# Own products with values in three pieces, and all products with values a tick later

## The chip, the cores and the metric

The kernel runs on one core of a Trainium2 chip. A core has five engines that run beside each other, each with its own program: TensorE (PE, matmuls; its weight loads are shown apart as PEld), VectorE (DVE), ScalarE (ACT), GpSimd (POOL) and SyncE (SP, which here does nothing but issue DMAs). They wait for each other on semaphores. The metric is the device time of one execution in microseconds (us).

## The reference

Block-sparse attention for 4 batches and 8 heads, 768 tokens of width 64 in blocks of 32 (so 24 blocks), with three drawn blocks of keys for each block of queries and a window of one block; then a mixture of eight experts on its output, 3072 tokens of 512, one expert for each token.

```python
scores = scale * np.matmul(q, k.transpose(0, 1, 3, 2))
...
mask = np.abs(blk_i - blk_j) <= window
mask = mask | (blk_i == 0) | (blk_j == 0) | (blk_i == n_blocks - 1) | (blk_j == n_blocks - 1)
for qb in range(n_blocks):
    for kb in sampled_blocks[qb]:
        mask[qb * block:(qb + 1) * block, kb * block:(kb + 1) * block] = True
scores = np.where(mask, scores, -1000000000.0)
scores = scores - np.max(scores, axis=-1, keepdims=True)
attn = np.exp(scores)
attn = attn / (np.sum(attn, axis=-1, keepdims=True) + 1e-09)
return np.matmul(attn, v).astype(np.float32)
...
for e in range(E):
    mask = e_idx == e
    if not mask.any():
        continue
    h = np.maximum(x[mask] @ w1[e], 0.0)
    out[mask] = gate_w[mask, None] * (h @ w2[e])
```

## The kernel before

Attention comes first, then the experts, whose first groups are begun while attention ends.

*Tiles and items.* The first and the last block of queries see all keys; they are worked on as "dense" items (kind "d"), 8 for each half of the batches. The other 22 blocks make 11 pairs, so with two halves there are 22 tiles of 128 tokens: two blocks (n) of two batches (b), for 8 heads. Each tile is four items of kind "s", one for each n and b. A block of queries sees eight blocks of keys. Four of them it shares with the other block of its tile (first, last, and the two of the tile's own pair): their values are the "shared" ones. The other four (three drawn ones and the neighbour outside the pair) are its "own".

*Ticks.* All items stand in one list, and in each tick `t` every step of the pipeline works on the item that is `LAG` ticks back; `ORDER` says in which order the steps stand within a tick. The steps are letters:

- S: scores on TensorE (L532, for both batches at once); M: mask and least value on VectorE (L540); X: exponential on ScalarE (L548)
- T: transposition of the weights on TensorE (L557); A: its copy out of the PSUM bank on ScalarE (L562); with a tile's last item also the sums' spreading on VectorE (L566)
- W: products of weights and shared values on TensorE (L579), into a new bank; the loop has 16 matmuls with 64 columns of weights each
- V: the sums of the rows by heads (L572, another bank), then the products with own values (L588): 32 matmuls with 32 columns each, into the bank that W began, four of them (j) for each of 8 heads
- O: division by the sums on VectorE (L439 to L441), which frees both banks; Y: turning of the result on TensorE (L595) and its copy by ScalarE (L597); G: gate logits on TensorE (L605), and after them the routing

W, V, O, Y and G work once for each tile, with its last item. For sparse items the lags of W, V, O, Y and G are 5, 7, 8, 10 and 13. Dense items have lags of their own, with a step W of their own (L430, L432). The order of every engine's program is the order in which this loop writes it: nothing is put elsewhere afterwards. An engine that waits holds up all that stands behind it on that engine.

*Values.* Two buffers hold a tile's values in turn (`vbuf[g % 2]`). For tile g SP loads two new neighbouring blocks (L495, L496; the first pairs also L490 to L493), and the drawn blocks of the two queries' blocks, three each (L520); GpSimd copies what the tile before has already (L503). `VL`, `VS` and `VG` say when: so many ticks after the last item of tile g-2, which used the same buffer, and at which of the eight places of a tick. Places 0 to 6 stand ahead of the steps O, X, T, S, M, A and W, place 7 at the tick's end. The load of q for a tile (`KL`, L143) and the writing of finished rows (`XD`, L1235) go through SP too, at place 2 and place 7.

*Banks.* PSUM has eight banks; attention takes them from one pool of eight.

*Records.* The trace shows two matmul records for each fp32 matmul of the program, but one for each transposition, and as many weight loads.

Of the kernel before, what the change touches and what calls it, by code (L numbers as in the profile page):

```python
# [38 lines left out]
HB = 2  # L39
# [21 lines left out]
ADVANCE = (((2, 3), (6, 6), (7, 1)), ((0, 2), (1, 1), (6, 4)))  # L61
LHS = (6, 5)
LHS_DVE = (True, True)
CHOOSE = ((0, 2),)
# [1 line left out]

KL = (-2, 2)
QP = (-2, 2)
VL = (8, 1)
VS = (11, 7)  # L70
VG = ((9, 6), (10, 3))

# [16 lines left out]
def attention_moe(ctx, tc, kD, qD, qH, v0, v1, blocks, modality, w_gate, bias, w1, w2, out):  # L89
# [29 lines left out]
    with ExitStack() as actx:  # L119
# [459 lines left out]
                    nc.tensor.matmul(o[64 * b:64 * b + 64, D * h:D * h + D], lhsT=a[b][:, 8 * u + 4 + pr].rearrange("p n q -> p (n q)"),  # L579
                                     rhs=vg[:, 1, b * HD + D * h:b * HD + D * h + D], start=h == 0, stop=False, tile_position=(0, 64 * b))  # L580

        def weigh_own(g, o, a):
            vg = vbuf[g % 2]
            for h in range(H):
                pr, u = divmod(h, 2)
                for j in range(4):
                    b, n = divmod(j, 2)
                    nc.tensor.matmul(o[32 * j:32 * j + 32, D * h:D * h + D], lhsT=a[b][:, 8 * u + pr, n],  # L588
                                     rhs=vg[:, 2 * n, b * HD + D * h:b * HD + D * h + D], start=False, stop=h == H - 1, tile_position=(0, 32 * j))
# [690 lines left out]
        def do(op, it):  # L1280
# [29 lines left out]
            else:  # L1310
# [20 lines left out]
                elif (n, b) == (1, HB - 1):  # L1331
# [16 lines left out]
        with man:  # L1348
# [16 lines left out]
            while t < NI + LAG["s"]["G"] + 1 or fillers or slots_todo or choosers or early:  # L1365
                spot = 0
                for op in ORDER:
                    if op in "TSMAXOW":
                        hook(spot)
                        spot += 1  # L1370
                    for kind in "ds":
                        k = t - LAG[kind][op]
                        if 0 <= k < NI and items[k][0] == kind:
                            do(op, items[k])
                hook(7)
                if t >= NI:
                    tail[0], tail[1] = t >= NI + TAIL, t >= NI + LAG["s"]["V"]
# [66 lines left out]
```

## Time and profile before

| | us |
|---|---|
| median of 3 runs | 537.08 |
| lowest and highest of them | 534.24, 539.2 |
| the profiled execution, its own time | 536.03 |
| its span, first to last instruction | 534.3 |

The mean granted TensorE clock of the profiled execution is 0.987 of full speed. The second part of the page cuts the span into 40 slices of 13.4 us; a digit is the busy share in tenths:

```profile
PE   7999999998999999899999999999999999999995
PEld 5667776766778777788989898998989899898984
DVE  7995698683788999867997656556565655656553
ACT  4689877884988878835456554546555454655552
POOL 3577685574468884323155022030302203030213
PEclk9999999997999999899999999999999999999998
```

Attention takes the first 17 slices. There TensorE, VectorE and ScalarE are all busy most of the time, and behind it TensorE nearly alone. The row PEclk shows the granted clock.

A matmul's end is modelled in such a trace, so a busy TensorE may still lose time between matmuls of different shapes: what counts is the time from one start to the next.

### The profile page before, as it was taken

To read this page: it belongs to the slowest core of one execution; us is meant where nothing else is said; L and a number is where in the kernel's file an instruction comes from. 1 tells how busy PE (TensorE), PEld (TensorE's weight loads), DVE (VectorE), ACT (ScalarE), POOL (GpSimd) and SP (SyncE) were. 2 spreads that over 40 slices of the span, in tenths; PEclk is the share of its full clock that TensorE was granted. 3 is DMA by queue.
4 is the path that set the end of the run, shared out by engine and by line. 5 is a ranking of instruction groups with operands and counts; after the bars stand their busy time and mean duration, and the time that the engine had idled before them with its cause. 6 is when DMAs were issued, how large, how long until landed. Compare 5 with 4: busy or idle time off the path is not lost.

```text
span 534.3 us, 19017 instructions
## 1 busy us (share of the span) xinstructions
PE 514.9 (96%) x7298; PEld 436.1 (82%) x7298; DVE 377.2 (71%) x1139; ACT 335.2 (63%) x765; POOL 214.9 (40%) x451
## 2 busy tenths in 40 slices
PE   7999999998999999899999999999999999999995
PEld 5667776766778777788989898998989899898984
DVE  7995698683788999867997656556565655656553
ACT  4689877884988878835456554546555454655552
POOL 3577685574468884323155022030302203030213
PEclk9999999997999999899999999999999999999998
DMA  7995887898846798965888686676758677675840
GB/s 278 339 234 153 238 244 224 243 229 223 232 126 194 198 231 252 274 193 200 238 288 303 227 261 200 237 252 202 244 177 261 203 227 242 213 246 180 257 155 23
DMA packets 49443, 119.44 MB, mean 224 GB/s; under 512 B 7744, under 2 KB 8128, under 8 KB 49344
## 3 DMA queue, kind: packets, MB, share of 16 engines
q1 hardware_dynamic: 45248, 105.02, 64.5%
q0 software_dynamic: 4096, 13.12, 7.3%
q8 instruction: 59, 0.97, 0.8%
q14 instruction: 40, 0.33, 0.2%
HBM read 105.52 MB, written 12.86 MB: 222 GB/s over the span
## 4 chain that ended last, share of the span: by engine, by line
issue 40%; PE 39%; DVE 7%; DMA 6%; POOL 6%; SPq 2%; ACT 1%; POOLq 0%; DVEq 0%; ACTq 0%
PE bank L557 7%; PE bank L532 6%; PE bank L579 4%; PE bank L588 4%; POOL slot L735 3%; DMA out<-slot,si 2%; DMA slot<-kD 2%; PE bank L605 2%; POOL out L789 2%; PE bank L595 2%; DVE y L540 2%; PE bank L753 1%; PE bank L769 1%; PE bank L770 1%; PE bank L768 1%
## 5 line engine op out<-in xcount | busy, mean ns | idle before, releaser
L724 DVE TENSOR_TENSOR slot<-slot 128x1024 fp32r<-128x1024 f32 x99 | 123.1, 1248 | 89.3 <-ACT slot L721 87.5
L721 ACT CAST slot<-slot 128x1024 fp32r<-128x1024 f32 x104 | 108.1, 1048 | 102.1 <-PE bank L754 52.1
L753 PE MATMUL bank<-slot 128*128 128x256 f32 x384 | 108.4, 282 | 0.0
L755 PE MATMUL bank<-slot 128*128 128x256 f32 x384 | 107.8, 281 | 0.0
L754 PE MATMUL bank<-slot 128*128 128x256 f32 x384 | 107.7, 280 | 0.0
L789 POOL DMA_INDIRECT out<-slot,si x20 | 25.4, 1270 | 178.6 <-ACT slot L785 175.6
L548 ACT ACTIVATE a<-y,mn 128x256 f32<-128x256 f32 x176 | 88.7, 511 | 7.7 <-DVE mn L540 7.6
L768 PE MATMUL bank<-slot 128*128 128x512 f32 x192 | 76.6, 399 | 0.0
L769 PE MATMUL bank<-slot 128*128 128x512 f32 x192 | 75.9, 395 | 0.0
L770 PE MATMUL bank<-slot 128*128 128x512 f32 x192 | 75.8, 395 | 0.0
L753 PEld LDWEIGHTS bank<-slot 128*128 128x128 f32 x384 | 72.3, 188 | 0.6
L754 PEld LDWEIGHTS bank<-slot 128*128 128x128 f32 x384 | 72.1, 188 | 0.4
L755 PEld LDWEIGHTS bank<-slot 128*128 128x128 f32 x384 | 72.2, 188 | 0.0
L540 DVE CUSTOM_DVE_ANT_1 y<-bank,smask 128x256 f32<-128x256 f32 x176 | 66.3, 416 | 0.6 <-PE bank L532 0.2
L481 POOL COPY slot<-slot 128x128 f32 x264 | 63.9, 294 | 0.0
L562 ACT COPY at<-bank 128x512 f32<-128x512 f32 x88 | 50.6, 576 | 12.8 <-PE bank L557 12.7
L557 PE MATMUL bank<-ident,a 128*128 128x128 f32 x352 | 52.8, 284 | 0.6 <-ACT a L400 0.5
L503 POOL TENSOR_SCALAR slot<-slot 32x1024 f32<-32x1024 f32 x40 | 41.9, 1048 | 28.0 <-PE bank L588 10.2
L532 PE MATMUL bank<-slot,q_raw 64*32 64x256 f32 x1408 | 48.8, 382 | 1.1 <-DMA q_raw<-qH 0.7
L770 PEld LDWEIGHTS bank<-slot 128*128 128x128 f32 x192 | 36.1, 188 | 8.4
L557 PEld LDWEIGHTS bank<-ident,a 128*128 128x128 f32 x352 | 38.9, 142 | 4.7 <-ACT a L548 0.8
L769 PEld LDWEIGHTS bank<-slot 128*128 128x128 f32 x192 | 36.1, 188 | 7.8 <-DVE slot L724 0.4
(302 smaller groups left out, 855.4 us busy)
## 6 DMA issues: line engine op xcount, KB each, us to landing
slot<-w SPq DMA_DIRECT2D x100, 512.0 KB, 4.0
slot<-v SPq DMA_DIRECT2D x180, 128.0 KB, 4.0
x_d<-xr SPq DMA_DIRECT2D x22, 256.5 KB, 5.3
q_raw<-qH SPq DMA_DIRECT2D x22, 256.0 KB, 4.8
slot<-v SPq DMA_DIRECT2D x16, 256.0 KB, 4.9
slot<-kD SPq DMA_DIRECT2D x13, 256.0 KB, 4.2
slot<-v SPq DMA_DIRECT2D x4, 768.0 KB, 11.9
slot<-w SPq DMA_DIRECT2D x10, 256.0 KB, 5.1
```

Of the source, the lines that this page charges most:

```text
L532: nc.tensor.matmul(sp[u][32 * pr:32 * pr + 32, b * 256:(b + 1) * 256], lhsT=q[r, b * NPAIR + pr, n, :], rhs=kv[r, s0:s0 + 8, b, pr, :], st ...
L540: nc.vector.tensor_tensor_reduce(y[:, u, :].rearrange("p (s f) -> p s f", s=8), sp[u][:, b * 256:(b + 1) * 256].rearrange("p (s f) -> p s ...
L548: nc.scalar.activation(a[:, u, :], y[:, u, :], AF.Exp, bias=mn[:, u:u + 1], scale=-1.0, accum_out=total[:, u:u + 1])
L557: nc.tensor.transpose(tp[:, k:k + P], a[:, u, c * P:(c + 1) * P], ident)
L721: nc.scalar.copy(h, s)
L724: (eng or (nc.gpsimd if n in POOL_SPLITS else nc.vector)).tensor_tensor(l, s, h.bitcast(F32), ALU.subtract)
L753: nc.tensor.matmul(o, lhsT=h[:, fs], rhs=xh[g % 2][:, c, :], start=c == 0 and f % 2 == 0, stop=False)
L754: nc.tensor.matmul(o, lhsT=h[:, fs], rhs=xl[g % 2][:, c, :], start=False, stop=False)
L755: nc.tensor.matmul(o, lhsT=l[:, fs], rhs=xh[g % 2][:, c, :], start=False, stop=c == 3 and f % 2 == 1)
L768: nc.tensor.matmul(o, lhsT=hh[0][:, f, ts_], rhs=h[:, fs], start=f == 0, stop=False)
L769: nc.tensor.matmul(o, lhsT=hh[0][:, f, ts_], rhs=l[:, fs], start=False, stop=False)
L770: nc.tensor.matmul(o, lhsT=hl[f // 4][:, f % 4, ts_], rhs=h[:, fs], start=False, stop=f == 7)
```

## The change

Sparse items get a third step with values, U. Own products are divided by heads: heads 0 and 1 in step W behind the shared products, heads 2 and 3 in step U, and heads 4 to 7 in step V behind the row sums. The steps of a tile move a tick later: W from 5 to 6, U at 7, V from 7 to 8, O from 8 to 9, Y from 10 to 11. G stays at 13. The very last item keeps its old ticks (`LAST`), with U between W and V. The load of new neighbouring blocks moves from place 1 to place 7 of its tick, since V now reads the old ones within that tick. The number of matmuls, copies and DMAs is the same.

```diff
-LAG = {'d': {'S': 0, 'M': 1, 'X': 2, 'T': 4, 'A': 4, 'W': 7, 'O': 8, 'V': 101, 'Y': 11, 'G': 13}, 's': {'S': 0, 'M': 1, 'X': 2, 'T': 4, 'A': 4, 'W': 5, 'V': 7, 'O': 8, 'Y': 10, 'G': 13}}
-ORDER = 'OXTSMGVAYW'
+LAG = {'d': {'S': 0, 'M': 1, 'X': 2, 'T': 4, 'A': 4, 'W': 7, 'O': 8, 'V': 101, 'Y': 11, 'G': 13}, 's': {'S': 0, 'M': 1, 'X': 2, 'T': 4, 'A': 4, 'W': 6, 'U': 7, 'V': 8, 'O': 9, 'Y': 11, 'G': 13}}
+LAST = {'W': 5, 'U': 6, 'V': 7, 'O': 8, 'Y': 10}
+OWN = {'W': (0, 2), 'U': (2, 4), 'V': (4, 8)}
+ORDER = 'OXTSMGVUAYW'
...
-VL = (8, 1)
+VL = (8, 7)
...
-        def weigh_own(g, o, a):
+        def weigh_own(g, o, a, heads):
             vg = vbuf[g % 2]
-            for h in range(H):
+            for h in range(*heads):
...
                         sum_rows(sums.pop((m, half)), banks[m, half])
-                        weigh_own(half * NM + m, st[it], [ats[m, half, b_] for b_ in range(HB)])
+                    if op in OWN:
+                        weigh_own(half * NM + m, st[it], [ats[m, half, b_] for b_ in range(HB)], OWN[op])
...
-                        k = t - LAG[kind][op]
+                        k = t - LAG[kind].get(op, NEVER)
                         if 0 <= k < NI and items[k][0] == kind:
                             do(op, items[k])
+                    if op in LAST and t - LAST[op] == NI - 1:
+                        do(op, items[NI - 1])
```

In the changed file these lines stand three further on (L579 is L582 there, L588 is L591, L595 is L598).

On TensorE, for one full tile from its shared products on, the order before is this; the names are the bank written, the weights and the moving operand, the size is that of the output, and x is the number of equal matmuls in a row:

```order
L579 MATMUL bank<-slot,at 64x64 x16
L557 MATMUL bank<-ident,a 128x128 x4
L595 MATMUL bank<-ident,xr 128x128 x4
L557 MATMUL bank<-ident,a 128x128 x4
L532 MATMUL bank<-slot,q_raw 32x256 x16
L572 MATMUL bank<-rexp,fold 32x8 x4
L588 MATMUL bank<-slot,at 32x64 x32
L557 MATMUL bank<-ident,a 128x128 x8
L532 MATMUL bank<-slot,q_raw 32x256 x16
L605 MATMUL bank<-wg_raw,xT 64x8 x8
```

After the change the same engine reads, for the same stretch:

```order
L582 MATMUL bank<-slot,at 64x64 x16
L591 MATMUL bank<-slot,at 32x64 x8
L560 MATMUL bank<-ident,a 128x128 x4
L535 MATMUL bank<-slot,q_raw 32x256 x16
L591 MATMUL bank<-slot,at 32x64 x8
L598 MATMUL bank<-ident,xr 128x128 x4
L560 MATMUL bank<-ident,a 128x128 x4
L575 MATMUL bank<-rexp,fold 32x8 x4
L591 MATMUL bank<-slot,at 32x64 x16
L560 MATMUL bank<-ident,a 128x128 x4
L535 MATMUL bank<-slot,q_raw 32x256 x16
L608 MATMUL bank<-wg_raw,xT 64x8 x8
```

The 32 own matmuls stand in three places instead of one, and each of them has transpositions behind it; four more transpositions follow the gate's matmuls.

On SP, in the first half of attention, the DMAs from a writing of finished rows on are in this order before:

```order
L1235 DMA x_d<-xrd 128x513
L495 DMA slot<-v 32x1024
L496 DMA slot<-v 32x1024
L143 DMA q_raw<-qH 128x512
L512 TENSOR_LOAD rb_i
L520 ISA
```

and after the change:

```order
L1238 DMA x_d<-xrd 128x513
L146 DMA q_raw<-qH 128x512
L515 TENSOR_LOAD rb_i
L498 DMA slot<-v 32x1024
L499 DMA slot<-v 32x1024
L523 ISA
```

The two loads of new blocks, which wait for own products, now stand behind the load of q and the reading of the drawn blocks' numbers instead of ahead of them. On VectorE the division (L439 to L441) stands a tick later among the masks. GpSimd's order is the same in both.

More of the change, by code (lines that the diff above doesn't have):

```diff
@@ L58 @@
 DENSE_AFTER = (21, 29, 45, 47)
[L59 to L60 removed]
+LAG = {'d': {'S': 0, 'M': 1, 'X': 2, 'T': 4, 'A': 4, 'W': 7, 'O': 8, 'V': 101, 'Y': 11, 'G': 13}, 's': {'S': 0, 'M': 1, 'X': 2, 'T': 4, 'A': 4, 'W': 6, 'U': 7, 'V': 8, 'O': 9, 'Y': 11, 'G': 13}}
+LAST = {'W': 5, 'U': 6, 'V': 7, 'O': 8, 'Y': 10}
+OWN = {'W': (0, 2), 'U': (2, 4), 'V': (4, 8)}
+ORDER = 'OXTSMGVUAYW'
 ADVANCE = (((2, 3), (6, 6), (7, 1)), ((0, 2), (1, 1), (6, 4)))
+NEVER = 1000
 LHS = (6, 5)
@@ L1371, in attention_moe @@
                     for kind in "ds":
-                        k = t - LAG[kind][op]
+                        k = t - LAG[kind].get(op, NEVER)
                         if 0 <= k < NI and items[k][0] == kind:
                             do(op, items[k])
+                    if op in LAST and t - LAST[op] == NI - 1:
+                        do(op, items[NI - 1])
                 hook(7)
                 if t >= NI:
-                    tail[0], tail[1] = t >= NI + TAIL, t >= NI + LAG["s"]["V"]
+                    tail[0], tail[1] = t >= NI + TAIL, t >= NI + LAST["V"]
                     for _ in range(2):
```

## The prediction

> **What bounds the kernel now.** I read the page first, then the busy times by stage, then the chain of work that ended last in order of time, and last TensorE's two timelines (its matmuls, and its weight loads, where a wait shows before it shows on the matmuls).
>
> The page gives engines and DMA queues:
>
> ```profile
> PE 514.9 (96%) x7298; PEld 436.1 (82%) x7298; DVE 377.2 (71%) x1139; ACT 335.2 (63%) x765; POOL 214.9 (40%) x451
> ...
> q8 instruction: 59, 0.97, 0.8%
> ```
>
> TensorE is busy 96% of the span, and queue 8 brought 59 packets of code. The trace holds 7298 matmuls and as many weight loads; 14,596 over 59 is 247 for each packet. So q8 carries TensorE's own code, one packet for some 250 instructions.
>
> Attention fills some 195 us, up to its last own products (L588) at 230.29 (row below), the experts the rest. What a tile of 128 tokens costs there is read from the chain of work, in order of time (start, length, what), in a stretch where no piece waits:
>
> ```profile
> 165.24 0.98 PE bank L579 x32
> 166.22 0.59 PE bank L557 x4
> 166.81 0.44 PE bank L595 x4
> 167.25 0.44 PE bank L557 x4
> 167.68 1.02 PE bank L532 x32
> 168.71 0.18 PE bank L572 x8
> 168.88 0.92 PE bank L588 x64
> 169.80 1.02 PE bank L557 x8
> 170.82 1.02 PE bank L532 x32
> 171.85 0.57 PE bank L605 x16
> ```
>
> Each piece begins where the one ahead ends, all of it on TensorE: 7.18 us for a tile, with nothing of another engine in between. So in attention TensorE's own time is the path, and a nanosecond added to it is a nanosecond of the kernel. The rows also give a price that is needed below: four transpositions cost 0.59 as the first of a run, the next four 0.44, and a run of eight 1.02. A run of transpositions that is begun anew thus costs 0.15 us (0.59 less 0.44) beyond its work.
>
> TensorE does stop in places. The matmul timeline shows two long stops, each in the middle of one run of equal matmuls:
>
> ```profile
> 121.60 1.65 PE L579 MATMUL bank<-slot,at 128*64 128x64 f32 x25 [2.65 <-issue]
> ...
> 215.14 1.11 PE L588 MATMUL bank<-slot,at 128*32 128x64 f32 x48
> 218.07 0.43 PE L588 MATMUL bank<-slot,at 128*32 128x64 f32 x16 [1.83 <-issue]
> ```
>
> The weight loads show three short ones of the same kind, the first at 100.97:
>
> ```profile
> 100.97 0.54 PEld L432 LDWEIGHTS bank<-slot 128*64 128x64 f32 x14 [0.33 <-issue]
> ...
> 211.53 0.83 PEld L579 LDWEIGHTS bank<-slot,at 128*64 128x64 f32 x25 [0.42 <-issue]
> ...
> 230.29 1.06 PEld L588 LDWEIGHTS bank<-slot,at 128*32 128x32 f32 x63 [0.52 <-issue]
> ```
>
> They wait for nothing that the profile shows, and they fall inside a run. What else needs time there is the engine's code. The busy times by stage (columns: window, length, then each engine's busy time with its count, granted clock, DMA share) bear it out:
>
> ```profile
> 121.59:218.00 96.41, 93.53 (x2398) 72.53 (x2399) 78.06 (x381) 79.96 (x255) 61.20 (x167) 0.97 0.76 210
> ...
> 120.90:127.80 6.90, 6.20 (x49) 4.54 (x53) 0.38 (x4) 3.20 (x10) 3.68 (x15) 0.51 1.02 264
> 219.90:223.30 3.40, 3.40 (x47) 3.28 (x44) 2.74 (x10) 1.58 (x6) 1.59 (x2) 0.50 1.07 309
> ```
>
> Between the two long stops lie 2398 + 2399 instructions, 19 packets of 252: the stops stand a whole number of packets apart. The other two rows show what a long stop brings with it. Right behind each, the granted clock is half for 6.9 and for 3.4 us, which loses 3.4 and 1.7 us more. The stops above sum to 2.65 + 1.83 + 0.33 + 0.42 + 0.52 = 5.75 us, the clock to 5.1: together 10.9 us of attention that aren't work.
>
> The Trainium skill's page "Runtime: NRT & Kernel Launch", section "Instruction fetch mechanics", says that each engine's code is refilled in blocks of 256 instructions by its own queue, and that crossing a block's end is mostly hidden. The size agrees with the 247 to 252 above, the hiding doesn't: by that rule the 2.65 us would have another cause and the change would save nothing of it (rival 1).
>
> **The change, part by part.**
>
> *Own products in three pieces.* In a full tile (its rows of the order stand ahead, in the part on the change) the 64 own matmul records (L588) stood in one run; now 16 stand behind the shared products (L579), 16 behind the second half's scores (L532), 32 behind the row sums (L572). Because the pieces now stand between transpositions, these are parted too: of two runs in a tile (8, and 4+4+4 with the turning) come four. Counted over the whole order of both programs, own runs go from 22 to 65 (+43), transposition runs from 62 to 104 (+42); nothing else is added. A transposition run costs 0.15: 42 x 0.15 = 6.3 us.
>
> For an own run the trace has one length only, so its price is bounded. The weight loads around one, the next ones being those of the turning:
>
> ```profile
> 161.08 0.95 PEld L588 LDWEIGHTS bank<-slot,at 128*32 128x32 f32 x64
> 162.12 0.42 PEld L595 LDWEIGHTS bank<-ident,xrd 128*128 128x128 f32 x4
> ```
>
> The last own load ends at 162.03, the next begins at 162.12: 0.09 us at the run's end is the lower bound. The upper one comes from the gate's 16 records (L605): 0.57, where own work at 0.92 / 64 would take 0.23 for 16, so 0.34. I take 0.13, next to the 0.15 of the transpositions, since both change between the shape 128*128 and a narrow one: 43 x 0.13 = 5.6 us (3.9 to 14.6). Switches sum to +11.9 us, about 0.55 for each tile, all of it on the path.
>
> *Code comes more evenly.* A packet is asked for while the one ahead of it is worked off, so what counts is how fast 250 instructions (two for each record) can go. Before, the densest stretch was scores (64 instructions, 1.02), row sums (16, 0.18), own (128, 0.92), eight transpositions (16, 1.02) and half the next scores (32, 0.51): 256 in 3.65 us. Now it is scores (64, 1.02), own (32, 0.23 + 0.13), eight transpositions (16, 1.02), sums (16, 0.18), own (64, 0.46 + 0.13), four transpositions (8, 0.59) and most of the scores (56, 0.89): 256 in 4.65. Each packet has up to 1.0 us longer to come. The two long stops shrink to 1.65 and 0.83, the short ones vanish: -3.3 us, between 0 (the packets come late by something that grows) and -5.75 (none is late).
>
> *Clock.* With 1.65 us the first stop is near the 1.83 that cost one stretch of 3.4 us at half speed; the other falls to 0.83, nearer the 0.52 that cost nothing. I keep one such stretch, 1.7 us, of 5.1: -3.4 us, between 0 and -5.1.
>
> *Everything a tick later.* Shared products, sums and division wait a tick longer for what they read. These waits of TensorE were ahead of them; the fifth row is L572 in the tile without waits, where 0.41 of idle weight loading is usual, so only what is above that counts for L572, and the last is the copy of a bank by ScalarE:
>
> ```profile
> 38.61 0.72 PEld L579 LDWEIGHTS bank<-slot,at 128*64 128x64 f32 x22 [0.64 <-ACT at L562]
> ...
> 57.15 0.16 PEld L572 LDWEIGHTS bank<-rexp,fold 128*32 128x32 f32 x8 [0.75 <-DVE mn L540]
> ...
> 69.12 1.04 PEld L579 LDWEIGHTS bank<-slot,at 128*64 128x64 f32 x32 [0.38 <-POOL slot L503]
> ...
> 198.57 0.16 PEld L572 LDWEIGHTS bank<-rexp,fold 128*32 128x32 f32 x8 [0.86 <-ACT at L562]
> ...
> 168.63 0.16 PEld L572 LDWEIGHTS bank<-rexp,fold 128*32 128x32 f32 x8 [0.41 <-ACT xT L597]
> ...
> L562 ACT COPY at<-bank 128x512 f32<-128x512 f32 x88 | 50.6, 576 | 12.8 <-PE bank L557 12.7
> ```
>
> 0.64 + 0.34 + 0.38 + 0.45 = 1.8 us, which a tick (7.18 / 4 = 1.8 us) covers: -1.8. What is nearer now: the gate stays at its tick while the turning moves, so that from the turning's first transposition to the gate TensorE has 0.59 + 0.44 + 0.18 + 0.59 + 0.59 + 1.02 = 3.4 us of work (before 0.44 + 0.44 + 1.02 + 0.18 + 0.92 + 1.02 + 1.02 = 5.0), in which ScalarE must copy the turned tile; the copy of a bank takes 0.58 us there, and ScalarE is 63% busy. I put +0.8 for this and for scores that take a bank which the division has just left, between 0 and 3.
>
> *Loads.* No DMA is added. The fetch of two new blocks of values (L495, L496) must wait for the own products, so it moves by the same tick and now stands behind the load of q on SP's queue instead of ahead of it. These are the waits there, and how long such a load takes:
>
> ```profile
> SPq L495 <- PE bank L588: 11.6, 4, 5.2
> ...
> slot<-v SPq DMA_DIRECT2D x180, 128.0 KB, 4.0
> ```
>
> SP waited 11.6 us in 4 places for own products, with the q load queued behind it; that one is now ahead, and a later wait of SP holds up the own blocks behind it alone. From the last own product of a tile to the shared products that need the new blocks there are six ticks, 10.8 us, and a load takes 4.0: hidden. GpSimd's copy of shared values (L503) keeps its place three ticks behind. Cost 0; if the cover went, the first shared product would wait for a landing as at 69.12, 0.4 us a tile.
>
> *The last tile* keeps its old ticks, so the hand-over to the experts stays where it was: 0.
>
> *Sum:* +11.9 - 3.3 - 3.4 - 1.8 + 0.8 = +4.2 us. The profiled execution took 536.03 (span 534.3 and 1.7 around it): 540.2. The median of the runs shown, 537.08, lies 1.05 above it, so I expect 541.3 us.
>
> **The rivals.**
>
> 1. *Code comes as late as before: slower still.* If the late packets are late because the DMA engines are full (DMA share 1.02 in the row of 120.90), not because TensorE is quick, another 1.0 us need not help, and the stops land elsewhere at their old size. Then +11.9 - 1.8 + 0.8 = +10.9, that is 548.0. For it: the 2.65 is far beyond the 1.0 that is won. Against: three of five stops are below 1.0. The Trainium skill's rule on fetching leads to the same time.
>
> 2. *Faster: the dense own run was the cause of all stops.* If no packet is late any more, all 10.9 go, and with an own run at its lower bound the switches cost 6.3 + 3.9 = 10.2: 10.2 - 10.9 - 1.8 = -2.5, that is 534.6. Only if own runs cost nothing at all does it reach 6.3 - 10.9 - 1.8 = -6.4, 530.7, beyond 1%. Its place is the two long stops; it decides once the new order wins 2.65 us for a packet, against the 1.0 that I count.
>
> 3. *Nothing.* TensorE's switches hide in its waits: 537. Against it: the chain above has no wait to hide in.
>
> For rivals 1 and 2 the clock matters. The Trainium skill's page "TensorE: Matmul & The Clock Gate", part 1, has the clock fall after about 3.4 us of idleness; here it fell behind 2.65 and 1.83, so the trace disagrees. By the page no stop of the new order would cost clock, and the sum would be 1.7 lower.
>
> **How the numbers follow.** Chances: my forecast, between 537 and 545, 0.64; rival 1, up to 549, 0.18; rival 2 0.12; rival 3 0.06. The range of 8 in 10 reaches from 535 (rival 2) to 547.5 (most of rival 1). About 1% is what a measurement here can tell from no change, 531.7 to 542.5. Above it lie rival 1 and the upper third of the forecast, 0.18 + 0.22 = 0.40; below it the outer half of rival 2, 0.06; the rest, 0.54, is within.
>
> **What would show it.** In the new chain of work a full tile should read near 7.75 us with transpositions of 0.59 four at a time and own pieces near 0.35, 0.35 and 0.6: right or wrong at once. Stops by issue inside a run should sum to 2 to 3 us, and the windows should show at most one stretch at half clock. Were own pieces 0.25, the switches would be half; were there stops of 2 us and more, rival 1 holds. TensorE waiting for the division ahead of scores, or for ScalarE ahead of the gate, in every tile would make all of it wrong upward.

## The result, and the profile after

| | before | after |
|---|---|---|
| median of 12 runs each, us | 538.95 | 543.21 |
| lowest and highest, us | 534.24, 542.96 | 540.28, 544.95 |
| ratio, with its 95% interval | | 1.0102 [1.0073, 1.013] |
| profiled execution, span | 536.03, 534.3 | 544.95, 543.2 |

The changed kernel takes 1% longer. Its profiled execution was its slowest run, that of before lay under its median, so the two spans differ by 8.9 us where the medians differ by 4.3 and the ratio makes 5.5 (0.0102 x 538.95). Medians are of all executions of a kernel, ratios of those within 1.5% of its fastest, so the two can differ a little.

The page's row of engines, after:

```profile
PE 526.1 (97%) x7298; PEld 436.0 (80%) x7298; DVE 377.9 (70%) x1139; ACT 335.9 (62%) x765; POOL 214.3 (39%) x451
```

TensorE is busy 11.2 us longer with the same 7298 matmuls; the other engines do what they did. The chain of work after, in order of time (start, length, what), for one full tile without waits, from one gate (L608) to the next:

```profile
167.70 0.57 PE bank L608 x16
168.27 0.59 PE bank L560 x4
168.85 1.08 PE bank L582 x32
169.94 0.36 PE bank L591 x16
170.30 0.59 PE bank L560 x4
170.88 1.02 PE bank L535 x32
171.91 0.36 PE bank L591 x16
172.27 0.59 PE bank L598 x4
172.85 0.44 PE bank L560 x4
173.29 0.18 PE bank L575 x8
173.47 0.47 PE bank L591 x32
173.94 0.59 PE bank L560 x4
174.53 1.02 PE bank L535 x32
```

From 167.70 to the end of the last row, 174.53 + 1.02 = 175.55, the tile takes 7.85 us, where it took 7.18. Own products are 0.36 + 0.36 + 0.47 = 1.19 instead of 0.92, four runs of transpositions begin at 0.59, and the shared products take 1.08 instead of 0.98, now that transpositions stand ahead of them.

The weight loads show two short stops, the first at the end of a run of own products, the second inside one, and the matmul timeline shows the long one (what stands in brackets is the idle time ahead, and what ended it):

```profile
75.77 0.31 PEld L598 LDWEIGHTS bank<-ident,xr 128*128 128x128 f32 x3 [0.77 <-issue]
...
130.60 0.14 PEld L591 LDWEIGHTS bank<-slot,at 128*32 128x32 f32 x2 [0.65 <-issue]
```

```profile
226.78 0.54 PE L591 MATMUL bank<-slot,at 128*32 128x64 f32 x24 [2.56 <-issue]
```

And the busy times by stage (window, length, busy time of each engine with its count, clock, DMA share) show the clock around the last one:

```profile
120.90:127.80 6.90, 6.62 (x164) 4.55 (x164) 5.57 (x25) 6.14 (x21) 5.92 (x15) 1.00 0.88 247
215.70:224.00 8.30, 7.80 (x173) 5.30 (x173) 6.79 (x36) 6.18 (x20) 0.96 (x1) 1.00 0.91 237
224.00:226.80 2.80, 0.24 (x19) 0.12 (x13) 2.10 (x10) 2.80 (x8) 1.94 (x2) 1.00 0.46 139
226.80:231.30 4.50, 4.50 (x56) 4.09 (x55) 3.81 (x10) 2.40 (x8) 2.22 (x3) 0.63 0.99 286
```

The long stop at 121 is gone (full clock at 120.90). The second has grown from 1.83 to 2.56 us; it lies at 224 now, ahead of the same packet of code as before (the 39th of queue 8), and behind it the clock falls once.

To compare all runs, attention is cut here from the first shared products to the end of the last own ones, and every matmul's distance to the next is set against what the same step usually takes. What exceeds it by over 0.15 us is counted as a stop of code if it stands at the place that returns every 256 TensorE instructions (the stops that the prediction lists all stand there), as loss at half clock if it lies in a stretch of half clock, and as a wait otherwise; all else is TensorE's own time. Runs are counted as the trace shows them in that stretch, the turning's transpositions with the scores'. Each row is one execution, the profiled one, while the ratio is of many; e1 to e12 are the experiments below. What is called usual moves the terms by an us or so: with medians of each kernel alone, after less before is 10.2 us of own time, -2.7 of code, -2.1 of half clock and +2.3 of waits, where the table makes 11.6, -4.0, -2.8 and +2.9.

| | runs: transposing, own | own time, us | code | half clock | waits | attention | ratio |
|---|---|---|---|---|---|---|---|
| before | 54, 22 | 174.8 | 8.6 | 4.0 | 6.2 | 193.6 | 1 |
| after | 95, 66 | 186.4 | 4.6 | 1.2 | 9.1 | 201.3 | 1.010 |
| e1 two pieces, old ticks | 54, 44 | 177.3 | 4.0 | 2.4 | 14.1 | 197.8 | 1.005 |
| e2 three pieces, old ticks | 75, 65 | 184.0 | 5.4 | 3.8 | 10.5 | 203.7 | 1.009 |
| e3 later, one run | 94, 22 | 180.7 | 5.4 | 0 | 11.4 | 197.4 | 1.013 |
| e4 before, half own work | 54, 22 | 165.4 | 1.3 | 0.8 | 18.3 | 185.8 | 0.986 |
| e5 after, half own work | 95, 45 | 176.5 | 0 | 0.6 | 15.4 | 192.5 | 1.009 |
| e6 before, loads' place | 54, 22 | 174.2 | 10.8 | 2.8 | 8.8 | 196.7 | 1.002 |
| e7 two pieces, two later | 53, 47 | 174.7 | 5.3 | 2.4 | 15.6 | 198.0 | 1.017 |
| e8 one run, two later | 53, 22 | 171.8 | 9.6 | 2.7 | 18.6 | 202.6 | 1.021 |
| e9 as e7, gate later | 51, 45 | 174.3 | 1.0 | 4.9 | 17.8 | 198.0 | 1.032 |
| e10 after, weights held | 95, 67 | 186.4 | 2.0 | 0 | 8.6 | 197.0 | 1.019 |
| e11 ahead, two pieces | 75, 44 | 179.8 | 1.3 | 1.2 | 14.6 | 196.8 | 1.006 |
| e12 ahead, one run | 75, 22 | 177.5 | 8.4 | 2.7 | 6.8 | 195.5 | 1.003 |

In e7, e8 and e9 the stretch begins 3 us later (41 us instead of 37 to 38), with 3 us of the work already done.

### The profile page after: what moved, and what is told of

It is laid out like the page before. It is cut to its first block, busy times and chain, and to the rows that moved or that the text cites. A ratio compares the mean times of both kernels' runs of the same rounds, so it can differ in the third digit from the quotient of the medians.

```text
span 543.2 us, 19041 instructions
## 1 busy us (share of the span) xinstructions
PE 526.1 (97%) x7298; PEld 436.0 (80%) x7298; DVE 377.9 (70%) x1139; ACT 335.9 (62%) x765; POOL 214.3 (39%) x451
## 3 DMA queue, kind: packets, MB, share of 16 engines
q1 hardware_dynamic: 45248, 105.02, 63.2%
## 4 chain that ended last, share of the span: by engine, by line
issue 39%; PE 37%; DMA 6%; POOL 6%; DVE 4%; SPq 4%; ACT 1%; POOLq 1%; ACTq 0%; DVEq 0%
PE bank L535 7%; PE bank L560 6%; PE bank L591 4%; PE bank L582 3%; POOL slot L738 3%; DMA out<-slot,si 2%; PE bank L598 2%; PE bank L608 2%; POOL out L792 2%; DMA slot<-v 2%; PE bank L772 1%; PE bank L756 1%; PE bank L773 1%; PE bank L771 1%; DMA q_raw<-qH 1%
## 5 line engine op out<-in xcount | busy, mean ns | idle before, releaser
L560 PE MATMUL bank<-ident,a 128*128 128x128 f32 x352 | 56.6, 285 | 0.7 <-ACT at L565 0.3
L535 PE MATMUL bank<-slot,q_raw 64*32 64x256 f32 x1408 | 51.2, 382 | 2.9 <-DMA q_raw<-qH 1.1
```

What stands on the lines that cost most here:

```text
L535: nc.tensor.matmul(sp[u][32 * pr:32 * pr + 32, b * 256:(b + 1) * 256], lhsT=q[r, b * NPAIR + pr, n, :], rhs=kv[r, s0:s0 + 8, b, pr, :], st ...
L560: nc.tensor.transpose(tp[:, k:k + P], a[:, u, c * P:(c + 1) * P], ident)
```

## The experiments

Diffs of e1 to e3, e5, e7, e8 and e10 to e12 are against the changed kernel, of e4 and e6 against the kernel before, of e9 against e7. They are cut to the lines that matter: where a kernel has other steps, `LAST` changes with them, of a changed `LAG` often the new line alone is shown, and e4 and e5 also set the flag `stop` at the last head that is left.

**e1, e2: the pieces without the later tick.**

In both the lags go back to those of before; e1 has two pieces (heads 0 to 3 in W, 4 to 7 in V), e2 the three of the change. Against the changed kernel, e1:

```diff
-LAG = {'d': {'S': 0, 'M': 1, 'X': 2, 'T': 4, 'A': 4, 'W': 7, 'O': 8, 'V': 101, 'Y': 11, 'G': 13}, 's': {'S': 0, 'M': 1, 'X': 2, 'T': 4, 'A': 4, 'W': 6, 'U': 7, 'V': 8, 'O': 9, 'Y': 11, 'G': 13}}
+LAG = {'d': {'S': 0, 'M': 1, 'X': 2, 'T': 4, 'A': 4, 'W': 7, 'O': 8, 'V': 101, 'Y': 11, 'G': 13}, 's': {'S': 0, 'M': 1, 'X': 2, 'T': 4, 'A': 4, 'W': 5, 'V': 7, 'O': 8, 'Y': 10, 'G': 13}}
-OWN = {'W': (0, 2), 'U': (2, 4), 'V': (4, 8)}
+OWN = {'W': (0, 4), 'V': (4, 8)}
-VL = (8, 7)
+VL = (8, 1)
```

and e2:

```diff
+LAG = {'d': {'S': 0, 'M': 1, 'X': 2, 'T': 4, 'A': 4, 'W': 7, 'O': 8, 'V': 101, 'Y': 11, 'G': 13}, 's': {'S': 0, 'M': 1, 'X': 2, 'T': 4, 'A': 4, 'W': 5, 'U': 6, 'V': 7, 'O': 8, 'Y': 10, 'G': 13}}
-VL = (8, 7)
+VL = (8, 1)
```

> Own products in two pieces (heads 0 to 3 with the shared products, 4 to 7 with the row sums), all steps at the old ticks. Transposition runs stay at 62, own runs go from 22 to 44. Theory A (each run begun anew costs TensorE 0.13 to 0.15 us, and spread code comes less late): +22 x 0.13 = +2.9 us of switches, less 2 to 5 us of late code: -2 to +1 us against the kernel before, own pieces of 0.59 each in the chain. Theory B (the tick later is what costs, splitting is free): -3 to -6 us. Theory C (switches cost, late code is not helped): +2.9 us.

> The change's three own pieces, but all steps at the old ticks. Transposition runs 62 to 83, own runs 22 to 65. Theory A: +21 x 0.15 + 43 x 0.13 = +8.7 us of switches, less 3 to 5 of late code: +4 to +6 us. Theory B: -3 to -6 us, since no step is a tick later. Theory C: +8 to +9 us.

e1: 540.76 against 538.21, ratio 1.0048 [1.002, 1.0076], some 2.6 us: above theory A's range, at the value of theory C, though not by C's way, since its stops of code fell from 8.6 to 4.0 us. e2: 543.53, ratio 1.0092 [1.0058, 1.0126], some 5.0 us, as theory A has it. TensorE's own time rises as the runs do: e1 by 2.5 us for 22 more own runs (0.11 each), e2 by 9.2 for 21 more of transpositions and 43 more own. But new waits come. The weight loads of e2 and e1:

```profile
65.28 0.26 PEld L591 LDWEIGHTS bank<-slot,at 128*32 128x32 f32 x14 [3.14 <-DMA slot<-v]
```

```profile
203.74 0.16 PEld L575 LDWEIGHTS bank<-rexp,fold 128*32 128x32 f32 x8 [2.90 <-DVE mn L543]
```

Own values read up to two ticks earlier had not landed (3.14 us, and half clock behind it in e2), and the row sums waited for VectorE (2.90). So these waits are what a later tick could spare. In the change it did little: its waits are 9.1 us against e2's 10.5, and its ratio is no better (1.0102 against 1.0092).

**e3: the later tick without the pieces.**

```diff
+LAG = {'d': {'S': 0, 'M': 1, 'X': 2, 'T': 4, 'A': 4, 'W': 7, 'O': 8, 'V': 101, 'Y': 11, 'G': 13}, 's': {'S': 0, 'M': 1, 'X': 2, 'T': 4, 'A': 4, 'W': 6, 'V': 8, 'O': 9, 'Y': 11, 'G': 13}}
-OWN = {'W': (0, 2), 'U': (2, 4), 'V': (4, 8)}
+OWN = {'V': (0, 8)}
```

> The tick later alone: own products in one run with the row sums as before, steps W, V, O, Y at the changed ticks. Own runs stay at 22, transposition runs go from 62 to 103, because the later steps stand between transpositions that were neighbours. Theory A: +41 x 0.15 = +6.2 us, less 1 to 2 of data waits that a tick covers and 0 to 1 of late code (the own run is as dense as before): +3 to +5 us, and no wait in every tile. Theory B: the same size, but as waits of TensorE for the gate's copy, the division or loads, tile by tile. Theory C: +4 to +5 us.

546.57 against 538.21, ratio 1.0128 [1.0076, 1.0179], some 6.9 us and more than any of the three theories had (its profiled execution, 542.17, was among its fastest). Own products stand in one run, yet transposition runs rise from 54 to 94 and own time by 5.9 us, 0.15 each. Scores come every second tick, transpositions every tick; before, everything else on TensorE stood in the ticks that have scores (but for the turning), and two ticks' transpositions met. One tick further on, shared and own products stand in the ticks between, and part them. So a large part of the price of the change belongs to the odd shift, not to the pieces. The rest of the 6.9 us is not in the switches: in the profiled execution waits rose from 6.2 to 11.4 us, while stops of code fell from 8.6 to 5.4.

**e4, e5: less own work.** In both the own products of heads 4 to 7 are left out.

e4, against before:

```diff
-            for h in range(H):
+            for h in range(H // 2):
```

e5, against after:

```diff
-OWN = {'W': (0, 2), 'U': (2, 4), 'V': (4, 8)}
+OWN = {'W': (0, 2), 'U': (2, 4), 'V': (4, 4)}
```

> The kernel before without the own products of heads 4 to 7 (their half of the output lacks these products). The own run goes from 64 records (0.92 us in the chain) to 32 (0.47), so the work left out is 22 x 0.45 = 9.9 us. Theory A (the stops by issue are code that comes late, because the own run empties a packet too fast): the densest 256 instructions take some 4.3 us instead of 3.65, so some of the stops and the half clock go too: -13 to -15 us. Rival (the stops have another cause, spread code wins nothing): the work alone, -9 to -11 us.

> The changed kernel without the own products of heads 4 to 7, that is without the third piece (their half of the output lacks these products). Work left out: 22 x 0.47 = 10.3 us against the changed kernel, which itself is 4 to 5 us above the kernel before. Theory A: the code was spread already, so little more comes with it, -10 to -12 against the changed kernel, that is -5 to -8 against the kernel before, and 7 to 9 us above the kernel before without the same products (nearly the whole price of the switches shows). Rival: the distance between the two without these products stays at 4 to 5 us.

e4: 528.31 against 535.85, ratio 0.9861 [0.9821, 0.9902], 7.5 us for some 9.5 us of work left out, though stops of code and half clock went too (12.6 to 2.1 us). That is less than theory A and its rival had. e5: 540.2 against 535.85, ratio 1.0094 [1.0065, 1.0123]: next to nothing beside the 1.0102 of after, for some 10 us of work left out, and far from the 10 to 12 us of theory A. Waits take the place: 6.2 to 18.3 us in e4, and 9.1 to 15.4 in e5. For e5 they are not all of it, since in its profiled execution, one of its fastest, attention still is 8.8 us shorter than in after; what its other executions lost isn't shown. The chain of e5 at one of its two longest waits shows how (the other, at 230, is for own values):

```profile
86.21 0.59 PE bank L608 x16
86.82 0.18 DVE lg L611
87.02 0.18 DVE mx L297
87.23 0.19 DVE dl L300
87.44 0.94 DVE eq L305
88.40 0.17 DVE first L308
88.57 0.60 DVE nm L394
89.17 0.34 DVE nm L395
89.53 0.22 DVE nb__2354 L397
89.84 0.79 ACT a L403 x2
90.67 1.96 PE bank L535 x30
```

From the gate (L608) the path runs through VectorE's routing, then a dense item's mask and its exponential on ScalarE, back to scores on TensorE, which waits. In e4 the busy times of a stretch, against those of before:

```profile
45.00:215.00 170.00, 160.20 (x3693) 120.88 (x3690) 142.86 (x666) 145.25 (x465) 118.28 (x306) 0.99 0.85 228
```

```profile
45.00:215.00 170.00, 163.91 (x4209) 126.35 (x4193) 133.46 (x637) 140.45 (x453) 113.66 (x306) 0.98 0.78 218
```

VectorE, ScalarE and the DMA engines are at 79, 83 and 78% before, and at 84, 85 and 85% in e4: they are close behind TensorE, and a nanosecond taken from it is not always a nanosecond of the kernel.

**e6: the loads' new place alone, in the kernel before.**

```diff
-VL = (8, 1)
+VL = (8, 7)
```

> The kernel before with the load of new neighbouring blocks of values at the tick's end (place 7 instead of 1), behind the load of q on SP's queue; TensorE's order is unchanged. The prediction put the loads at 0: within 1 us of the kernel before, and no wait of TensorE for values. Rival (the loads' place is part of what the change costs): +1 to +3 us with waits for values ahead of shared products.

537.68 against 535.85, ratio 1.0022 [0.9986, 1.0058]: no difference that can be told, though the interval reaches to 3 us and does not shut out the rival's 1 to 3. Against the rival speaks that TensorE's matmuls wait in this trace for no DMA of values ahead of shared products.

**e7, e8: two ticks later, so that the shift is even.**

```diff
+LAG = {'d': {'S': 0, 'M': 1, 'X': 2, 'T': 4, 'A': 4, 'W': 7, 'O': 8, 'V': 101, 'Y': 11, 'G': 13}, 's': {'S': 0, 'M': 1, 'X': 2, 'T': 4, 'A': 4, 'W': 7, 'V': 9, 'O': 10, 'Y': 12, 'G': 13}}
-OWN = {'W': (0, 2), 'U': (2, 4), 'V': (4, 8)}
+OWN = {'W': (0, 4), 'V': (4, 8)}
-VL = (8, 7)
+VL = (9, 7)
```

is e7; e8 is the same with `OWN = {'V': (0, 8)}`, one own run.

> The changed kernel with its own products in two pieces (heads 0 to 3, heads 4 to 7) that come seven and nine ticks behind the scores, the output at ten and the turning at twelve: two ticks later than before, where the change has one. By the order of the instructions 63 runs of score transpositions (before 62, changed kernel 104) and 44 runs of own products (before 22, changed kernel 65). Theory one, the price lies in runs that begin anew: of the 11.9 us of switches only the 22 more own runs at 0.13 us stay, 2.9 us, while what the pieces save on late code and half clock (6.7 us by the prediction) stays too, so 0 to 1 per cent faster than the kernel before, ratio 0.990 to 1.000. Theory two, the price lies in being later (tiles held longer, the gate and row stores later, more waits): slower than the changed kernel, ratio above 1.012. In the first run of the pieces without a later tick, loads not landed and row sums cost some 8 us of waits more than before; theory one needs these to be gone here.

> The kernel before with everything behind the copies two ticks later (own products with the shared ones at nine ticks behind the scores, output at ten, turning at twelve), own products in one run, the last tile as before. 63 runs of score transpositions, 22 of own products: no more switches than before. Beside it stands the earlier run with the one tick later, own products in one run, 103 runs of score transpositions, ratio 1.013. Theory one, switches are the price: this kernel lacks those, ratio 0.995 to 1.004, and the difference to the run with one tick is 41 runs at 0.15 us, 6 us. Theory two, lateness is the price: ratio 1.013 or more. Late code is not relieved by either theory, since the own run of 64 matmuls is whole: stops of code together 6 us or more.

e7: 545.44 against 537.01, ratio 1.0172 [1.0122, 1.0223]. e8: 548.39, ratio 1.0213 [1.0167, 1.0259]. Own time came as theory one has it (53 runs of transpositions, some 12 us less than after for e7, 3 of which are the later start), and the time as theory two has it: waits of 15.6 and 18.6 us. Stops of code in e8, with its own products in one run, are 9.6 us, as expected. One of e7's waits, in the chain of work:

```profile
223.19 0.68 ACT a L551 x3
223.87 0.93 ACT slot L724
224.80 0.48 ACT at L565
225.28 0.49 ACT xT L600
225.77 0.04 issue
225.82 0.64 PE bank L608 x16
```

The gate (L608) is now one tick behind the turning, whose copy (L600) is queued on ScalarE behind exponentials, a conversion of expert weights and a bank's copy: TensorE waited 2.07 us here, and 3.6 us in three places by the waits on L600 alone.

**e9: e7 with the gate two ticks later.**

Against e7:

```diff
-LAG = {'d': {'S': 0, 'M': 1, 'X': 2, 'T': 4, 'A': 4, 'W': 7, 'O': 8, 'V': 101, 'Y': 11, 'G': 13}, 's': {'S': 0, 'M': 1, 'X': 2, 'T': 4, 'A': 4, 'W': 7, 'V': 9, 'O': 10, 'Y': 12, 'G': 13}}
+LAG = {'d': {'S': 0, 'M': 1, 'X': 2, 'T': 4, 'A': 4, 'W': 7, 'O': 8, 'V': 101, 'Y': 11, 'G': 13}, 's': {'S': 0, 'M': 1, 'X': 2, 'T': 4, 'A': 4, 'W': 7, 'V': 9, 'O': 10, 'Y': 12, 'G': 15}}
-LAST = {'W': 5, 'V': 7, 'O': 8, 'Y': 10}
+LAST = {'W': 5, 'V': 7, 'O': 8, 'Y': 10, 'G': 13}
```

> The run with two pieces two ticks later, with the gate's products at fifteen ticks behind the scores where they stood at thirteen (last tile: thirteen as before). In that run TensorE had the nominal time of the kernel before plus 3 us, but waited 15.6 us (before 6.2), of which 6.3 us at the gate: for the copy of the turned tile on ScalarE, which was queued behind the exponentials and copies of the scores (2.1, 1.6, 1.6 us). Theory one, a step comes too close behind its copy: with three ticks from turning to gate again, as before the change, the waits at the gate fall below 1 us and the kernel to a ratio of 1.000 to 1.008. Theory two, ScalarE and VectorE are themselves late there and whatever stands next on TensorE takes over the wait: waits stay at 13 us or more, ratio 1.012 or more.

555.02 against 539.49, ratio 1.0319 [1.0259, 1.0378]. The gate's waits went, and others came: 17.8 us in attention, and one among the experts. The longest two of TensorE:

```profile
PE bank L337 <- DVE oh L310: 4.1, 1, 4.1
PE bank L337 <- DVE xr L444: 3.1, 1, 3.1
```

The 3.1 us lie at 208.36 in attention, the 4.1 at 262.18 among the experts, and behind both the clock is half (6.8 us from 208.3, 3.4 from 262.9). At 262.18 TensorE waits for the routing on VectorE. At 208.36 its routing products wait for VectorE's division (L444), and the division itself had stood 5.38 us for a DMA, the writing of an earlier tile's rows. In e9 such waits of VectorE for `x_d<-xr` are 13.9 us in 3 places; in no other kernel here are they above 0.2 us. So the time is that of theory two, but a good part of the cause is neither theory's: rows are written behind the gate's routing, so a later gate holds their place longer, and the division waits for it.

**e10: the changed kernel with early expert weights held until attention is over.**

```diff
-TICKS = (6, 9, 12)
+TICKS = (99, 99, 99)
```

> The changed kernel with the loads of the first experts' weights, which lie between 205 and 230 us among the last loads of values, held until the attention is over (the instructions of TensorE and GpSimd stay in the same order; three conversions of weights on ScalarE and VectorE move out of this stretch too). Theory one, crowded transfers make the code and the query tile late there: the stop of 2.75 us at 224, the wait of 1.93 us at 215.7 and the 3.4 us at half clock behind them go or shrink to 1 us together, so the attention ends 4 to 6 us earlier, and what the later weights cost behind it is seen apart, 0 to 6 us. Theory two, the code is late whatever else moves: a stop of 2 us or more stays between 205 and 240.

549.41 against 539.49, ratio 1.019 [1.014, 1.024]; but attention ended at 235.3 instead of 239.8 us. (One of its six executions took 1248.64 us, for a reason that nothing on record shows; it is not in the ratio.) The same windows as those of after above:

```profile
215.70:224.00 8.30, 8.03 (x209) 5.88 (x213) 6.76 (x31) 7.27 (x24) 2.09 (x2) 1.00 0.75 222
224.00:226.80 2.80, 2.60 (x60) 2.08 (x48) 2.64 (x12) 2.80 (x11) 2.08 (x2) 1.00 0.29 98
...
238.60:248.80 10.20, 7.88 (x43) 7.05 (x44) 3.75 (x4) 2.09 (x2) 0.00 (x0) 0.50 0.61 200
```

The DMA share ahead of 224 is 0.75 instead of 0.91, TensorE works through the place of the stop (2.60 of 2.80 us, where it was 0.24), and no clock is lost in attention. So theory one: with TensorE's order untouched, that packet of code came in time once transfers had moved. (Three conversions of weights left ScalarE and VectorE there as well, so the transfers are not the only thing that moved.) What the stop had cost did not come back as waits here: they are 8.6 us, against 9.1 in after. The price comes behind, and is more than the 0 to 6 us expected: after attention the experts take 9.5 us more (312.9 against 303.4), TensorE waiting for converted weights, with a stretch of 10.2 us at half clock.

**e11, e12: pieces written ahead of the transpositions of their tick.** The tick is that of the change; steps U and V stand before T, so that two ticks' transpositions meet again.

e11, in which the step that begins a tile's shared products is called U:

```diff
+LAG = {'d': {'S': 0, 'M': 1, 'X': 2, 'T': 4, 'A': 4, 'W': 7, 'O': 8, 'V': 101, 'Y': 11, 'G': 13}, 's': {'S': 0, 'M': 1, 'X': 2, 'T': 4, 'A': 4, 'U': 6, 'V': 8, 'O': 9, 'Y': 11, 'G': 13}}
-OWN = {'W': (0, 2), 'U': (2, 4), 'V': (4, 8)}
+OWN = {'U': (0, 4), 'V': (4, 8)}
-ORDER = 'OXTSMGVUAYW'
+ORDER = 'OXVUTSMGAYW'
...
-                    if op == "W":
+                    if op == "U":
                         st[it] = bank()
```

e12 is the same with `OWN = {'V': (0, 8)}`.

> The changed kernel's later tick, with two pieces (shared products and heads 0 to 3 at six ticks, heads 4 to 7 at eight) that are written ahead of the transpositions of their tick and not behind them, so that two ticks' transpositions stand together again: 54 runs of score transpositions (before 62, changed kernel 104) and 44 of own products (22, 65), turning and gate as in the changed kernel. Theory one, the price of the change is its runs that begin anew: against the changed kernel 50 runs fewer at 0.15 us and 21 fewer at 0.13 us, 10 us less of TensorE's time in the attention; ratio 0.990 to 1.002. Theory two, waits take the place of what TensorE saves (as where everything came two ticks later and the waits rose to 15.6 us): ratio 1.008 or more, with waits of 13 us or more in the attention.

> The same places as the run beside it, but the own products of a tile in one run of all heads: 54 runs of score transpositions, 22 of own products. Beside the other run it tells what the pieces alone do. Theory one, pieces spare late code: 22 fewer own runs save 2.9 us of TensorE, and stops for code and half clock are 5 us or more longer than with two pieces, so this kernel is 1 to 4 us slower than the run with two pieces. Theory two, pieces do nothing for the code: this kernel is 2 to 4 us faster than the run with two pieces.

e11: 539.64 against 536.26, ratio 1.006 [1.0021, 1.0098]. e12: 538.19, ratio 1.0026 [0.9989, 1.0062]. My 54 counted the scores' runs alone and set them beside numbers that hold the turning too. With the turning there are 75, 20 fewer than after, so with 22 fewer own runs 3.0 + 2.9 us of own time were to be saved and not 10; 6.6 were. Between the two theories e11 stays undecided: the waits are 14.6 us, as theory two has it, the ratio lies between theirs.

The pair is the cleanest test of what pieces do, since only the heads' division differs. With one run e12 has a long stop in its own products and 6.8 us of half clock behind it, in the matmul timeline and the window:

```profile
217.33 0.80 PE L591 MATMUL bank<-slot,at 128*32 128x64 f32 x18 [2.53 <-issue]
```

```profile
217.30:224.10 6.80, 6.77 (x74) 5.92 (x75) 4.45 (x12) 3.93 (x12) 4.16 (x4) 0.50 0.90 244
```

With two pieces e11 has stops of code of 1.3 us instead of 8.4, and 1.2 at half clock instead of 2.7. So pieces do spare 8.6 us of late code and clock. And 7.8 us of it come back as waits (14.6 against 6.8), with 2.3 us of switches on top. Two of these waits, in e11's weight loads:

```profile
121.81 0.55 PEld L608 LDWEIGHTS bank<-wg_raw,xT 128*64 128x64 f32 x16 [1.49 <-DVE rt L442]
122.85 0.28 PEld L582 LDWEIGHTS bank<-slot,at 128*64 128x64 f32 x6 [0.49 <-POOL slot L472]
```

TensorE comes to the gate, and to the next shared products, before VectorE and GpSimd are done. In time, neither theory came: e12 was to be 1 to 4 us slower or 2 to 4 us faster than e11, and its median is 1.5 us lower with intervals that overlap. What the stops and waits of the two say rests on one execution each.

## Why the prediction was right, and where it was not

*Switches: +11.9, measured 11.6* (186.4 less 174.8; the profiled spans differ by 8.9 in all). Counts and prices held: 41 more runs of transpositions in the stretch (42 in the whole program), own pieces of 0.36, 0.36, 0.47 against 0.35, 0.35, 0.6 foreseen, and a tile of 7.85 against 7.75. Pairs of kernels give the same prices: for a transposition run 0.15 (e3 less before, 40 runs) and 0.13 (e12 less before, 21), for an own run 0.11 (e1 less before, 22), 0.10 (e11 less e12, 22) and 0.13 (after less e3, 44). The Trainium skill's page "TensorEngine Tiling (Array Packing)", section "Tiling Modes", says that a change of tiling mode drains TensorE. A price of 0.10 to 0.15 us for each further run between other shapes fits that; whether the draining is all of it, no run here shows. But the prediction's reason for the transposition runs, "Because the pieces now stand between transpositions", is not the main one: the shift by one tick alone brings 40 (e3: 5.9 us with no piece at all), the three pieces alone 21 (e2), and both together no more than 41.

*Late code: -3.3, measured -4.0*, from 8.6 to 4.6 with the short gaps that my five rows had left out. That pieces spare late code is right (e11 against e12: 7.1 us less). That the stops are code, the trace shows directly, since it has the times of queue 8's packets. The stops stand at a place that returns every 256 instructions, a boundary. In before and after, TensorE passed no boundary of attention sooner than 1.26 us after a packet had landed, and at the three long stops it went on 1.28 to 1.36 us after.

The same times show why the long stops did not shrink by 1.0 us each. The quickest 256 instructions of attention took 3.7 us before and 4.2 after (foreseen: 3.65 and 4.65), so the new order won 0.5 us at the tightest place. The rest is the packet's own start. The transfer of a packet, about 1 us long, began some time after TensorE had passed the boundary ahead of the one that needs it: 1.3 us after it in before and 1.4 in after (medians), but 4.1 us at both long stops of before and 5.3 at the one of after, while the DMA engines were 0.93 to 1.01 busy. In e10 no packet began later than 2.9 us, and the stop was gone. So both the pace at which TensorE takes its code and the start of the packet set a stop. What held a late packet up is not shown; full DMA engines are the likely cause, as rival 1 had it.

By the prediction's own signs rival 1 is thus half right. A stop of 2 us and more was to be its sign, and one of 2.56 stood; the stops were to sum to 2 to 3 us, and they sum to 4.6. Its time of 548.0 did not come, because code and half clock together still fell by 6.8 us.

*Half clock: -3.4, measured -2.8*, with one stretch left, as said. The prediction charged the kernel before with 5.1 us for it, where the count above finds 4.0: the first stretch begins at 120.94 inside its stop, where TensorE idles anyway. The second does not stand right behind its stop either, but begins 1.85 us later, at 219.92.

*Waits: -1.0, measured +2.9.* This is the step that failed: "1.8 us, which a tick (7.18 / 4 = 1.8 us) covers: -1.8", and "+0.8 for this and for scores that take a bank which the division has just left". The four waits listed there did go, but they were only 1.8 of 6.2 us, and in the changed kernel 9.1 us of waits stand, at places I hadn't listed: scores at 92.2 and 215.7 (1.19 and 1.93 us), own products at 63.2 and 237.8 (0.80 and 0.95). Of the changed kernel, a row of the weight loads and one of TensorE's waits by what they wait for (us in total, times, longest):

```profile
63.94 0.26 PEld L591 LDWEIGHTS bank<-slot,at 128*32 128x32 f32 x14 [0.67 <-DMA slot<-v]
```

```profile
PE bank L591 <- DMA slot<-v: 1.0, 2, 0.5
```

Own values (L591 for slot<-v) were a load the prediction had at 0; here they are 1.0 us. The first piece reads them a tick earlier than the one run did; e1 and e2, whose first piece reads them two ticks earlier, have 2.6 and 3.0 us. The wait at 92.2 is for a dense item's exponential on ScalarE (L403) by the profile. For the 1.93 us the profile names no releaser; it is gone in e10 with the weights held, which speaks for transfers, but conversions on ScalarE and VectorE moved as well, so that stays open. TensorE waits for ScalarE ahead of the gate, which the prediction's +0.8 was for, did not come in after; they came in e7 (3.6 us).

*The loads' place and the last tile: 0.* e6 fits the first (1.0022, with 1 in its interval), within 3 us. The stretch behind attention took 303.4 us (302.8 before), so the second holds.

*The sum.* 11.6 - 4.0 - 2.8 + 2.9 = 7.7 us in the profiled pair, where 4.2 was forecast and the medians show 4.3, the ratio 5.5. A single execution's stops differ from run to run by about as much as the terms: before's own runs lie between 534.24 and 542.96. So the agreement of 4.2 with 4.3 to 5.5 is partly luck. The price of the switches is borne out by the pairs of kernels; the other terms rest on one execution of each kernel.

*The premise that "a nanosecond added to it is a nanosecond of the kernel"* fits roughly what is added (own time and attention: e2 9.2 and 10.1 us, e3 5.9 and 3.8), but not always what is taken away. Code, half clock and waits together are 18.8 us before, 14.9 after, 20.5 in e1, 20.4 in e4, 16.0 in e5, 17.1 in e11 and 17.9 in e12: one kind goes, another grows. Where steps stand two ticks later the sum is 23 to 31 us (e7 to e9), and in e10, with fewer transfers, 10.6, so it is no constant. What limits attention once TensorE is quicker is a mix (VectorE's routing, ScalarE's copies, loads of values); which of these binds first was not separated. Rival 2, that the stops would all go and the kernel with them become faster, fell in the changed kernel because 4.6 us of them stayed. e4 and e11, with next to no stops of code, show that it need not have come even without them: they have 8 to 12 us more of waits than before.

No version that does all the work and moves products is faster than the kernel before; e12 comes nearest (1.0026 [0.9989, 1.0062]). e11, with its own products in two pieces, lies below the change (1.006 against 1.0102), though the intervals overlap.

## What to carry to other kernels

Before dividing a run of narrow matmuls or moving a step by a tick, count the runs of each shape that the new order has: each new run cost 0.10 to 0.15 us here, and a shift by an odd number of ticks parted other runs that nobody had touched. A stop that is taken from the busiest engine is worth its time only if the next engines are ahead of it. Where they run at 78 to 85%, as here, it can come back as waits (7.8 of 8.6 us in e11 against e12), or not (e10, where attention kept the gain). So test such a change against a twin that differs in one thing (e11 and e12), because the profile of one execution has stops that vary by as much as the gain.

## What the runs showed of the hardware

- The long stops inside runs of products in before, after, e2 and e12 stood whole multiples of 256 TensorE instructions apart. One of 1.81 us in e3, with no releaser named either, did not; it came two weight loads into a run of own products, where e2 and e5 wait for own values. The Trainium skill's page "Runtime: NRT & Kernel Launch", section "Instruction fetch mechanics", has blocks of that size, which agrees, and crossings that are mostly hidden. In number that agrees too: of the 38 boundaries of attention 33 were passed in before, and 34 in after, without more than 0.25 us of idle weight loading that goes beyond the usual and has no releaser. At the others it was 0.3 to 2.8 us, while the DMA engines were 0.93 to 1.01 busy ahead of the three longest.
- The clock fell to half for 3.4 us, or two or three times that, around every single stop of TensorE's matmuls of 2.07 us (e7) or more in attention, and around none shorter than 1.0 us. In between no threshold shows: it fell behind one of 1.01 us (e11, at 121.81, with a shorter wait close behind it) and not behind one of 1.83 (e8, at 121.25).
- A step that reads a copy one tick behind its making can wait for all that is queued ahead of it on ScalarE: in e7 exponentials, a conversion of 0.93 us and a bank's copy of 0.48 us stood ahead of the small copy (0.49 us), and TensorE waited 2.07 us.
